# Two layers of attention and gated MLP on one core: where the second layer's weight sums are prepared, and the order of work in its fourth block

## The chip, the core and the metric

The kernel runs on one core of a Trainium2 chip. The core's engines are named as the profile names them: PE (TensorE, matmuls), DVE (VectorE), ACT (ScalarE), POOL (GpSimd) and SP (SyncE, which here issues DMAs). Each engine works through its own instructions in the order of the program and waits for others by semaphores. The metric is the device time of one execution in microseconds (us). Lower is better.

## The reference

```python
def _A_ref(x, wqkv, wo):                       # H = 16 heads, D = 448, Dh = 28
    q, k, v = ...                              # (x @ wqkv) cut in three, by heads
    scores = jnp.einsum("bhqd,bhkd->bhqk", q, k) * (Dh ** -0.5)
    o = jnp.einsum("bhqk,bhkd->bhqd", _softmax(scores), v)
    return o.transpose(...).reshape(B, S, D) @ wo
def _B_ref(x, w_gate, w_up, w_down):           # F = 1792
    return (_sigmoid(x @ w_gate) * (x @ w_up)) @ w_down

x = x + _A_ref(_layernorm(x), A_wqkv, A_wo)    # x is 1 x 2048 x 448, float32
x = x + _B_ref(_layernorm(x), B_w_gate, B_w_up, B_w_down)
x = x + _A_ref(_layernorm(x), A_wqkv, A_wo)    # the same weights again
x = x + _B_ref(_layernorm(x), B_w_gate, B_w_up, B_w_down)
```

## The kernel before, in words

The 2048 tokens are worked in four blocks of 512. A layer goes through four stages: `project` (layer norm, then q, k and v of each block), `attend` (scores, exponentials, products with the values, over 256 chunks: 16 heads by 16 key chunks), `out_project` (the output projection, the additions to x, the next layer norm) and `gated` (the MLP). Numbers in float32 are carried as a high and a low half-precision part, so most products are done as three.

**Two ways of projecting.** In the first layer q and k of a block come from `qk`: seven tiles of 128 features. For each tile PE makes the products (L618) into one of four banks; ACT reads out the high part (L871) and squares it (L874), DVE makes the low part (L872) and a maximum over halves of the squares (L878), SP stores q and k (L881), and PE adds up the squares by heads (L850 for q, L853 for k). That last product is held back by three tiles in a queue called `late`: after the products of the tile with index i come the norm products of the tile i - 3. After each tile `qk` calls a step of the list `fill`, in which other work of the kernel is put by hand. In the second layer the third and fourth block use `qk_sums` instead, a scheme of the Strassen kind on pairs of tiles. It multiplies with sums of quarters of the weight matrix rather than with the quarters themselves. Six tiles are taken as three pairs, `PAIRS_QK = ((0, 1), (4, 5), (2, 6))`; tile 3 is alone (`ALONE`) and is multiplied in the usual way into a bank named "alone". `qk_sums` returns `finish`, which does deferred squares one at a time when it is called with `whole=False`, and otherwise the last norm sums and the maxima over them (`peaks`, L1088).

**The weight sums.** They are prepared while the first layer runs. `read_pairs(js)` loads the float32 columns of the given pairs into a buffer `raws` with four DMAs a pair (L732, L734; POOL's queue) and a memset. The buffer has two halves: pairs 0 and 2 use one, pair 1 the other. `keep_pair(j)` makes the sums (`add_up`, four additions on DVE, L254), their high parts (ACT, L263; or DVE, L261, if it is named as the engine) and their low parts (DVE, L266), and POOL sends the pack to memory (L750), from where the second layer loads it. Pair 2 mixes two scales, so two scalings on DVE (L746) go ahead. Before, pairs 0 and 1 are read in the last steps of the second block's `qk`, and kept after the first and second tile of the third block's. Pair 2 is read after the third block's third tile and kept, all on DVE, at the start of attention.

**The input blocks.** A later block is normalized on DVE, stored by four DMAs to a scratch in memory (`store`, L391) and gathered in turned order by two (`gather`, L399 and L401), both on SP; `ready` then splits it. The fourth block's gather (`b3.gather`) stands at the first tile of the second block's values (`vals(1, ...)`).

**The guard.** After the fourth block's q and k, `guard_of_norms` (in the first layer called within the first tile of `vals(2, ...)`) takes a bound from the peaks, writes a guard row (DVE, L1228) and sends it off on POOL. `worst_of_heads` (L1235 to L1237) makes a flag from it; all engines load the flag and branch on it (L1244). After the branch SP loads the first heads, and the value products of the fourth block's last two tiles are done beside the first scores. DVE reads such a tile out (L1124).

**Attention and what follows.** In attention PE makes scores (L1529), ACT takes exponentials of three chunks at once (L1544), DVE does some by a polynomial, PE multiplies with the values (L1580). `along(c)` is called once a chunk and puts the preparation of other weights in. `out_project` makes six output products (into six banks), adds tails, and then DVE adds the first four tiles to x (`add`, L1713) and takes their statistics; PE's later products need the banks that these additions free.

Of the kernel before, what the change touches and what calls it, by code (L numbers as in the profile page):

```python
# [19 lines left out]
P = 128  # L20
# [101 lines left out]
def interleaved_layers(ctx: ExitStack, tc: tile.TileContext, x_in, wqkv, wo, w_gate, w_up,  # L122
                       w_down, out):
    nc = tc.nc
# [530 lines left out]
    class WeightsQKV:  # L655
# [66 lines left out]
            nc.sync.dma_start(v_parts, self.v)  # L722
            big.put(*self.qk, self.v)

        def read_pairs(self, js):
            self.raws = big.get("raws", [P, 2, 1024])
            self.to_add = len(js)
            for j in js:
                v = self.pair(j)
                for z, i in enumerate(PAIRS_QK[j]):  # L730
                    c = slice(i * P, (i + 1) * P)
                    nc.gpsimd.dma_start(v[:, 0:3, z],  # L732
                                        wqkv[0:384, c].rearrange("(s p) n -> p s n", p=P))
                    nc.gpsimd.dma_start(v[0:64, 3, z], wqkv[384:448, c])  # L734
                nc.gpsimd.memset(v[64:P, 3], 0.0)

        def pair(self, j):
            return self.raws[:, j % 2].rearrange("p (s z n) -> p s z n", s=4, z=2)

        def keep_pair(self, j, engine=None):  # L740
            v, t = self.pair(j), big.get("pack", [P, N_SUMS, P], F16)
            m = [int(i > ALONE) for i in PAIRS_QK[j]]
            by = up[:, m[0]:m[0] + 1]
            if m[0] != m[1]:
                for z in range(2):
                    nc.vector.tensor_scalar(v[:, :, z], v[:, :, z], up[:, m[z]:m[z] + 1], None,  # L746
                                            op0=ALU.mult)
                by = ones[:, 0:1]
            split_sums(t, v, by, engine)
            nc.gpsimd.dma_start(qs_parts[j], t)  # L750
            big.put(t)
            self.to_add -= 1
            if not self.to_add:
                big.put(self.raws)

        def load(self, j):
# [69 lines left out]
    def project(layer, wq, begun):  # L826
# [69 lines left out]
        def qk_sums(b, blk, points, before=None, defer=False):  # L896
# [21 lines left out]
            def at(i):  # L918
                for do in points.get(i, ()):
                    do()  # L920
# [105 lines left out]
            pa.third()  # L1026
            pb.third()
            at(2)
            if before:
                before(False)  # L1030
                before(False)
            pa.c11_c22()
            pb.c11_c22()
            at(3)
            pa.tiles[0].high()
            pa.c21()
            pa.tiles[0].low(pa.one)
# [1 line left out]
            pb.c21()  # L1039
            pb.tiles[0].low(pb.one)  # L1040
            pa.c12()
            if before:
                before()
            pb.c12()
            alone = bank(5 - b % 2, "alone")
            pc = Pair(2, 6)
            pc.first()
            pa.tiles[1].high()
            pa.tiles[1].low(pa.two)
            some(3)  # L1050
# [120 lines left out]
        if layer == 0:  # L1171
            fin = qk(0, blks[0], fill, None)
            vals(0, blks[0], along_values)
            fill = [b2.gather, b3.norm, sq(3, 0, 1), sq(3, 2, 3), idle,
                    lambda: b2.ready(0, 1), lambda: (b2.ready(2, 3), b3.store())]
            fill[4] = lambda: wq.read_pairs((0, 1))
            fin = qk(1, b1, fill, None)
            vals(1, b1, {0: b3.gather, 2: fin})
            add = tell.add
            fin = qk(2, b2, [lambda: wq.keep_pair(0),  # L1180
                             lambda: (wq.keep_pair(1), b3.ready(0, 1)),
                             lambda: (b3.ready(2, 3), wq.read_pairs((2,))), idle, add, add,
                             add], None)
            fin = qk(3, blks[3], [add, add, add], fin)
        else:
            ones_of_values()
            wq.load_usual()
            h2, h3, s3 = b2.half_steps(), b3.half_steps(), b3.squared()
            ready = [lambda kt=kt: b1.ready(kt) for kt in range(4)]
            both = lambda *steps: lambda: [do() for do in steps]  # L1190
            fin = qk_sums(0, blks[0], {0: ready[0:1], 1: ready[1:2], 2: s3[0:1],
                                       4: ready[2:3], 5: ready[3:4] + s3[1:2]})
            vals(0, blks[0], {0: both(s3[2], s3[3], s3[6], h2[0]), 1: both(s3[4], s3[7]),
                              2: both(fin, s3[5], s3[8], s3[9], b3.store),
                              3: both(h2[1], h2[2], b3.gather)})
            fin = qk(1, b1, h2[3:10], None)
            big.put(*wq.qk)
            vals(1, b1, {0: h3[0], 1: both(h3[1], h3[2], fin), 2: both(*h3[3:5]),
                         3: both(*h3[5:7])}, banks=(3, 0, 1, 6))
            fin = qk_sums(2, b2, {0: h3[7:8], 1: h3[8:9], 4: h3[9:10]}, None, True)  # L1200
            fin = qk_sums(3, b3, {}, fin)
        if layer > 0:
            big.put(*wq.held[1:])
            evac[0] = 0
        else:
            both_back(0, 0, 1, SCALE * 2.0 ** -20)
            nc.scalar.reg_load(exp_scale, back.bitcast(I32)[0:1, 0:1])
            nc.vector.tensor_scalar(base2, back[:, 0:1], math.log2(math.e), None, op0=ALU.mult)
# [11 lines left out]
        def guard_of_norms():  # L1220

            fin()
            heads[0].load()
            nc.vector.tensor_reduce(top, peaks, axis=AX.X, op=ALU.max)
            nc.vector.scalar_tensor_tensor(bnd, top[:, 0:1], SLACK, top[:, 1:2], op0=ALU.mult,
                                           op1=ALU.mult)
            nc.gpsimd.tensor_tensor(bnd, bnd, half[0:H, 0:1], op=ALU.pow)
            nc.vector.tensor_scalar(guard, zero, bnd, -1.0 / UNIT, op0=ALU.add, op1=ALU.mult)  # L1228
            nc.gpsimd.dma_start(g_scr[:, 0, :], guard)
            nc.gpsimd.dma_start(g_scr[:, 1, :], zero)  # L1230
            big.put(guard, zero)

        def worst_of_heads():
            pb = bank(4, "bounds")
# [15 lines left out]
        heads[0].load_guard()  # L1250
        heads[1].load()
        heads[1].load_guard()
        if layer == 0:
            wq.keep_pair(2, nc.vector)

        vals(3, blks[3], {}, [2], 0 if layer == 0 else 7)

        def last_values(begun=None):
# [239 lines left out]
                2 if half is None else half]  # L1498
            return self.kt[3][r, k, t * P:(t + 1) * P]

    def attend(layer, values, heads, last_values, gate, keep):
        new_banks()
        heads = list(heads)
        outs = Outputs()
# [87 lines left out]
        def along(c):  # L1592
            nonlocal prepare
            if layer == 0 and c == 2:
                keep()
            if layer == 0 and c == 4:
                prepare = Prepare()
            if prepare:
                prepare.along(c)
# [84 lines left out]
        return outs  # L1684


    def out_project(outs, gate):
        new_banks()
        nc.scalar.activation(warm, warm, AF.Sigmoid)
        nc.scalar.reg_load(gate_scale, back.bitcast(I32)[0:1, 3:4])  # L1690
# [25 lines left out]
        gate.load_gu()  # L1716
        gate.load_usual()
        products(range(6), range(6))
        first.begin()
        tails(range(4))  # L1720
        for t in range(4):
# [499 lines left out]
    for layer in range(LAYERS):  # L2221
        values, heads, last_values = project(layer, wq, begun)
        gate = WeightsGated()
        outs = attend(layer, values, heads, last_values, gate, wq.keep)
        mlp_first = out_project(outs, gate)
        wq = WeightsQKV()

        begun = gated(layer, mlp_first, gate, wq)
# [28 lines left out]
```

## Time and profile before

| what | value |
| --- | --- |
| median of three runs | 1900.61 us (1899.11 to 1901.45) |
| the profiled execution: its time | 1900.84 us |
| its span, first to last instruction | 1898.9 us |
| PE busy | 1882.1 us (99%) |
| DVE busy | 1480.3 us (78%) |
| ACT busy | 1422.5 us (75%) |
| POOL busy | 252.1 us (13%) |
| mean granted clock of PE | 0.998 |

The span is taken by the profiler within the execution; the execution's own time is 1.9 us longer. In a row of a timeline, the first number is the start in us from the span's beginning, the second the duration of the row (of all its instructions together, where it ends on xN), then come the engine, the line of the kernel, the operation, what it writes <- what it reads with the shape, the count, and in square brackets how long the engine had been idle before it and what it waited for. A q behind an engine's name (SPq, ACTq) marks its DMA issues. A row of the waits of PE gives the total wait, the number of waits and the longest. In a window's row the mean granted clock stands behind the busy times of PE, PEld (weight load), DVE, ACT and POOL.

### The profile page before, as it was taken

The numbers are of one execution on the slowest core, as the hardware profiler recorded it, in microseconds if no ns is written. First come the engines' busy times: TensorE is split into PE (matmuls) and PEld (weight loads), VectorE is DVE, ScalarE is ACT, GpSimd is POOL, SyncE is SP. The second block draws the span as 40 slices with busy tenths as digits, with TensorE's granted clock in tenths as the row PEclk, the third lists the DMA queues.
The fourth block names the chain that finished last, engine by engine and source line by source line (L and its number), as shares of the span: only waits on it lengthen the run. The fifth ranks groups of instructions, "written<-read, shape, count | busy, mean of one in ns | idle before, by whom it ended". The sixth has DMA issues, their size and how long they took to land. (4 is left out here: it accounts for less than half of the span.)

```text
span 1898.9 us, 57174 instructions
## 1 busy us (share of the span) xinstructions
PE 1882.1 (99%) x24531; PEld 1365.9 (72%) x24531; DVE 1480.3 (78%) x2988; ACT 1422.5 (75%) x1881; POOL 252.1 (13%) x489
## 2 busy tenths in 40 slices
PE   9999999999999999999999999999999999999999
PEld 4447756655565899999977566667666568999998
DVE  7858989898987887788867577787787688877664
ACT  5559999999993655555557899999999746555541
POOL 3313112122201211112110000000000021111110
PEclk9999999999999999999999999999999999999999
DMA  7775534434332755656573421122120246566553
GB/s 248 255 219 155 137 107 137 114 113 130 110 107 68 255 193 199 244 207 232 184 239 114 107 51 35 44 52 48 30 52 13 75 157 227 201 228 223 212 207 141
DMA packets 117335, 278.70 MB, mean 147 GB/s; under 512 B 14574, under 2 KB 72686, under 8 KB 116944
## 3 DMA queue, kind: packets, MB, share of 16 engines
q0 software_dynamic: 33680, 166.05, 24.2%
q1 hardware_dynamic: 82240, 107.53, 19.7%
q8 instruction: 194, 3.18, 0.7%
q10 hardware_dynamic: 1152, 1.38, 0.3%
q14 instruction: 69, 0.57, 0.1%
HBM read 213.43 MB, written 53.08 MB: 140 GB/s over the span
## 5 line engine op out<-in xcount | busy, mean ns | idle before, releaser
L1544 ACT ACTIVATE prob_s<-sc 128x1536 f32<-128x1536 f32 (+1 forms) x657 | 888.9, 1478 | 15.0 <-PE sc L1529 9.9
L1580 PE MATMUL acc<-prob_s,val_s 128*32 128x256 f32 (+3 forms) x7700 | 577.1, 384 | 1.6 <-issue 1.6
L1529 PE MATMUL sc<-qp_s 114*32 114x512 f16 x7868 | 559.9, 379 | 0.0
L633 PEld LDWEIGHTS <-gu_s 128*128 128x128 f16 x4368 | 426.8, 98 | 45.8 <-PE op L1709 0.7
L1529 PEld LDWEIGHTS <-qp_s 114*32 114x32 f16 x8192 | 283.4, 96 | 196.0 <-issue 85.5
L1580 PEld LDWEIGHTS acc<-prob_s,val_s 128*32 128x32 f32 x7700 | 284.1, 110 | 134.1 <-issue 13.6
L633 PE MATMUL chain<-xwide_s,gu_s 128*128 128x256 f16 x2016 | 247.6, 273 | 0.0
L1889 PE MATMUL dnp<-dn_s,hparts_s 128*128 128x224 f16 x2184 | 246.0, 259 | 0.2 <-DVE x L1907 0.2
L1889 PEld LDWEIGHTS <-hparts_s 128*128 128x128 f16 x2184 | 210.2, 98 | 5.5 <-issue 0.3
L1560 DVE SCALAR_TENSOR_TENSOR power_q<-power_q,expo_q 128x512 f32<-128x512 f32 x243 | 168.2, 692 | 8.3
L1962 ACT COPY one_q<-chain 128x256 f32<-128x256 f32 x224 | 82.3, 371 | 113.9 <-PE chain L633 113.4
L1978 DVE TENSOR_TENSOR one_q<-side,one_q 128x512 f32<-128x512 f32 x112 | 72.1, 686 | 95.8 <-PE side L633 95.6
L633 PE MATMUL side<-xshort_s,gu_s 128*128 128x256 f16 x1120 | 140.6, 273 | 0.0
L1770 POOL DMA_DIRECT2D gu_s<-gu_parts x104 | 56.0, 539 | 428.6 <-PE side L633 425.0
L1609 DVE STREAM_TRANSPOSE oturned_q<-acc 128x512 f32<-128x512 f32 x32 | 22.9, 717 | 100.5 <-PE acc L1580 100.4
L1842 ACT CAST hparts_s<-hsums_q 128x256 f16<-128x256 f32 (+1 forms) x152 | 71.5, 485 | 37.2 <-DVE hsums_q L1854 23.6
L1580 PE MATMUL acc<-power_q,val_s 128*32 128x256 f32 (+3 forms) x300 | 94.2, 396 | 0.0
L633 PE MATMUL side<-xwide_s,gu_s 128*128 128x256 f16 x672 | 91.7, 273 | 0.0
L618 PE MATMUL qkp<-xhl_s,wqk_s 128*128 128x512 f16 x385 | 86.7, 379 | 0.9 <-ACT wqk_s L235 0.6
L1989 ACT ACTIVATE one_q<-one_q 128x512 f32<-128x512 f32 x56 | 35.3, 631 | 63.9 <-DVE one_q L1978 63.6
L1554 DVE TENSOR_SCALAR expo_q<-aside,base 128x512 f32<-128x512 f32 x81 | 60.6, 748 | 22.7 <-PE aside L1529 22.3
L1846 DVE TENSOR_TENSOR hparts_s<-hsums_q,hparts_s 128x256 f16<-128x256 f32 (+1 forms) x152 | 72.8, 519 | 5.9 <-ACT hparts_s L1842 5.9
(262 smaller groups left out, 2398.8 us busy)
## 6 DMA issues: line engine op xcount, KB each, us to landing
gu_s<-gu_parts POOLq DMA_DIRECT2D x104, 800.0 KB, 5.9
dn_s<-dn_parts POOLq DMA_DIRECT2D x42, 784.0 KB, 7.5
qp_s<-qk_scr SPq DMA_DIRECT2D x96, 224.0 KB
gu_parts<-pack_s POOLq DMA_DIRECT2D x14, 800.0 KB, 3.8
xt_scr<-xs_s SPq DMA_DIRECT2D x48, 224.0 KB
xraw_s<-xt_scr SPq DMA_DIRECT2D x12, 768.0 KB
qk_scr<-qkhl_q SPq DMA_DIRECT2D x35, 256.0 KB
qp_s<-qk_scr SPq DMA_DIRECT2D x64, 112.0 KB
```

The lines of the kernel that those rows point to most:

```text
L618: nc.tensor.matmul(pm, w, x, start=(i == 0), stop=(i == len(terms) - 1))
L633: nc.tensor.matmul(pm, a, x, start=(first and i == 0), stop=(i == len(terms) - 1), skip_group_check=True)
L1529: nc.tensor.matmul(ps[32 * j:32 * j + 32, :], hd.k[:, keys], hd.q[:, qb * W:(qb + 1) * W], start=True, stop=True, tile_position=(0, 32 * j))
L1544: nc.scalar.activation(prob[:, 0:n, :], ps[:, 0:n, :], AF.Exp, scale=exp_scale)
L1554: nc.vector.tensor_scalar(y, ps, base2[:, 0:1], -126.0, op0=ALU.mult, op1=ALU.max)
L1560: nc.vector.scalar_tensor_tensor(p, p, c[k], y, op0=ALU.add, op1=ALU.mult)
L1580: nc.tensor.matmul(acc[qb * VC:(qb + 1) * VC, s], v[:, kc % TB, h, :], probs[c * NB + qb][:, s], start=(kc == 0 and a == 0), stop=(kc == N ...
L1842: nc.scalar.copy(to[:, :, 0], a)
L1846: nc.vector.tensor_tensor(to[:, :, 1], a, to[:, :, 0], op=ALU.subtract)
L1889: nc.tensor.matmul(pm, a[:, x, t], w[:, p, y], start=(begin and n == 0 and (j == 0 or alone)), stop=(n == 2), skip_group_check=True)
L1962: nc.scalar.copy(to, pm)
L1978: nc.vector.tensor_tensor(one[m], side[m], one[m], op=ALU.add)
```

## The change

In the first layer the three pairs are handled one by one, each at another place. Pair 0 is read on SP's queue at the second tile of the second block's values, behind the fourth block's gather, and kept as before after the third block's first tile. Pair 1 is read on SP after the fourth block's first tile and kept behind the guard. Pair 2 is read on POOL's queue six chunks before the end of attention and kept in `out_project`, behind the first six output products; its high parts go to ACT. In the second layer the half steps of the fourth block's input are dealt out differently over the steps around it; in the fourth block's `qk_sums` two deferred squares of the third block move behind `at(3)`, the third block's last norm sums and peaks move behind `pc.first()`, and the lone tile takes bank 0 instead of bank 4. The counter that hands out read-out banks starts at 1 instead of 0 behind it.

```diff
-        def read_pairs(self, js):
-            self.raws = big.get("raws", [P, 2, 1024])
-            self.to_add = len(js)
-            for j in js:
-                v = self.pair(j)
-                for z, i in enumerate(PAIRS_QK[j]):
-                    c = slice(i * P, (i + 1) * P)
-                    nc.gpsimd.dma_start(v[:, 0:3, z],
-                                        wqkv[0:384, c].rearrange("(s p) n -> p s n", p=P))
-                    nc.gpsimd.dma_start(v[0:64, 3, z], wqkv[384:448, c])
-                nc.gpsimd.memset(v[64:P, 3], 0.0)
+        def read_pair(self, j, queue=nc.sync):
+            if j != 1:
+                self.raws = big.get("raws", [P, 2, 1024])
+            v = self.pair(j)
+            for z, i in enumerate(PAIRS_QK[j]):
+                c = slice(i * P, (i + 1) * P)
+                queue.dma_start(v[:, 0:3, z], wqkv[0:384, c].rearrange("(s p) n -> p s n", p=P))
+                queue.dma_start(v[0:64, 3, z], wqkv[384:448, c])
+            nc.gpsimd.memset(v[64:P, 3], 0.0)
...
-        def keep_pair(self, j, engine=None):
+        def keep_pair(self, j):
...
-            split_sums(t, v, by, engine)
+            split_sums(t, v, by)
             nc.gpsimd.dma_start(qs_parts[j], t)
             big.put(t)
-            self.to_add -= 1
-            if not self.to_add:
+            if j > 0:
                 big.put(self.raws)
...
             at(2)
+            pa.c11_c22()
+            pb.c11_c22()
+            at(3)
             if before:
                 before(False)
                 before(False)
-            pa.c11_c22()
-            pb.c11_c22()
-            at(3)
...
             pa.c12()
+            pb.c12()
+            alone = bank(0 if before else 5, "alone")
+            pc = Pair(2, 6)
+            pc.first()
             if before:
                 before()
-            pb.c12()
-            alone = bank(5 - b % 2, "alone")
-            pc = Pair(2, 6)
-            pc.first()
...
-            fill[4] = lambda: wq.read_pairs((0, 1))
             fin = qk(1, b1, fill, None)
-            vals(1, b1, {0: b3.gather, 2: fin})
+            vals(1, b1, {0: b3.gather, 1: lambda: wq.read_pair(0), 2: fin})
             add = tell.add
             fin = qk(2, b2, [lambda: wq.keep_pair(0),
-                             lambda: (wq.keep_pair(1), b3.ready(0, 1)),
-                             lambda: (b3.ready(2, 3), wq.read_pairs((2,))), idle, add, add,
+                             lambda: b3.ready(0, 1), lambda: b3.ready(2, 3), idle, add, add,
                              add], None)
-            fin = qk(3, blks[3], [add, add, add], fin)
+            fin = qk(3, blks[3], [lambda: (add(), wq.read_pair(1)), add, add], fin)
...
-            vals(1, b1, {0: h3[0], 1: both(h3[1], h3[2], fin), 2: both(*h3[3:5]),
-                         3: both(*h3[5:7])}, banks=(3, 0, 1, 6))
-            fin = qk_sums(2, b2, {0: h3[7:8], 1: h3[8:9], 4: h3[9:10]}, None, True)
+            vals(1, b1, {0: both(*h3[0:2]), 1: both(h3[2], fin), 2: both(*h3[3:5]),
+                         3: h3[5]}, banks=(3, 0, 1, 6))
+            fin = qk_sums(2, b2, {0: h3[6:7], 1: h3[7:8], 3: h3[8:9], 4: h3[9:10]}, None, True)
...
-            evac[0] = 0
+            evac[0] = 1
...
             big.put(guard, zero)
+            if layer == 0:
+                wq.keep_pair(1)
...
-        if layer == 0:
-            wq.keep_pair(2, nc.vector)
-
         vals(3, blks[3], {}, [2], 0 if layer == 0 else 7)
...
+            if layer == 0 and c == total - 6:
+                wq.read_pair(2, nc.gpsimd)
...
         products(range(6), range(6))
+        if wq:
+            wq.keep_pair(2)
         first.begin()
```

`attend` and `out_project` are handed the object `wq` for this (`out_project` only in the first layer).

More of the change, by code (lines that the diff above doesn't have):

```diff
@@ L1499, in tail, with attend @@
             return self.kt[3][r, k, t * P:(t + 1) * P]
-    def attend(layer, values, heads, last_values, gate, keep):
+    def attend(layer, values, heads, last_values, gate, wq):
         new_banks()
@@ L1594, in along @@
             if layer == 0 and c == 2:
-                keep()
+                wq.keep()
+            if layer == 0 and c == total - 6:
+                wq.read_pair(2, nc.gpsimd)
             if layer == 0 and c == 4:
@@ L1684, in attend, with out_project @@
         return outs
-    def out_project(outs, gate):
+    def out_project(outs, gate, wq):
         new_banks()
@@ L2223, in interleaved_layers @@
         gate = WeightsGated()
-        outs = attend(layer, values, heads, last_values, gate, wq.keep)
-        mlp_first = out_project(outs, gate)
+        outs = attend(layer, values, heads, last_values, gate, wq)
+        mlp_first = out_project(outs, gate, wq if layer == 0 else None)
         wq = WeightsQKV()
```

## The prediction

> **What bounds the kernel.** I read the page first, then its waits of PE, the timelines of PE, DVE, ACT and SP around each edited place, the windows, and the pair buffer's tile view.
>
> ```profile
> span 1898.9 us, 57174 instructions
> PE 1882.1 (99%) x24531; PEld 1365.9 (72%) x24531; DVE 1480.3 (78%) x2988; ACT 1422.5 (75%) x1881; POOL 252.1 (13%) x489
> ```
>
> PE is busy but for 17 us, so an edit can count in three ways: it removes or adds a PE wait, it changes the granted clock, or it moves a stage that another engine paces. Attention is such a stage:
>
> ```profile
> 121.00:131.00 10.00, 6.55 (x47) 2.00 (x43) 4.28 (x10) 4.20 (x3) 0.57 (x1) 0.66 0.96 306
> 300.00:560.00 260.00, 260.00 (x4752) 154.80 (x4748) 233.58 (x458) 259.88 (x194) 50.48 (x86) 1.00 0.40 121
> ```
>
> The columns are length, then busy time of PE, PEld, DVE, ACT, POOL, then granted clock, DMA share, GB/s. In 300 to 560 ACT is busy 259.88 of 260, so a later or earlier start of ACT's exponentials carries through to the end of attention. In 121 to 131 PE works only 6.55 us and the mean clock is 0.66. The waits of PE that the edits touch:
>
> ```profile
> PE vp L643 <- DVE val_s L1124: 3.5, 1, 3.5
> PE qnorm L850 <- DVE sq_q L878: 1.0, 1, 1.0
> PE alone L1010 <- DVE peaks L1088: 0.6, 1, 0.6
> PE side L633 <- DVE one_q L984: 0.6, 1, 0.6
> PE chain L633 <- ACT one_q L968: 0.4, 1, 0.4
> ```
>
> **Part A: pair 2 leaves the start of attention, first layer.** Start, duration, engine, line:
>
> ```profile
> 113.52 0.16 DVE L1236 TENSOR_REDUCE worst<-bounds 1x1 f32<-1x16 f32 x1 [4.14 <-PE bounds L1235]
> 117.64 0.88 DVE L746 TENSOR_SCALAR raws_s<-raws_s,up 128x512 f32<-128x512 f32 x2 [3.71 <-DVEq L1244]
> 124.33 0.62 DVE L1124 TENSOR_SCALAR val_s<-vp 128x448 f32<-128x448 f32 x1
> 125.01 0.53 PE L643 MATMUL vp<-wv_s,xhl_s 128*128 128x448 f16 x1 [3.45 <-DVE val_s L1124]
> 120.96 2.79 ACT L1544 ACTIVATE prob_s<-sc 128x1536 f32<-128x1536 f32 x2 [2.62 <-DMA qp_s<-qk_scr]
> 128.86 1.45 ACT L1544 ACTIVATE prob_s<-sc 128x1536 f32<-128x1536 f32 x1 [5.11 <-PE sc L1529]
> 131.40 4.14 ACT L1544 ACTIVATE prob_s<-sc 128x1536 f32<-128x1536 f32 x3 [1.09 <-DMA qk_parts<-wqk_s]
> 1062.43 4.13 ACT L1544 ACTIVATE prob_s<-sc 128x1536 f32<-128x1536 f32 x3 [2.62 <-PE sc L1529]
> 1066.90 4.14 ACT L1544 ACTIVATE prob_s<-sc 128x1536 f32<-128x1536 f32 x3 [0.33 <-PE sc L1529]
> ```
>
> Pair 2's work (scalings, then L254, L261 and L266) holds DVE from 117.64 to 124.3; only then is the value tile read out (L1124), and PE waits 3.45 us for that bank. A clock of 0.66 over 10 us is 6.8 us at half speed, which slows the matmuls that follow too. The second layer has the same start without the sums: its fourth exponential begins 1066.90 - 1062.43 = 4.47 us after its first, against 131.40 - 120.96 = 10.44 here. The change makes the first layer like the second: 5.97 us earlier. Pair 1 now sits on DVE behind the guard, in an idle stretch before the flag; DVE is idle there for 4.14 us up to 113.52, that is from 109.4, and the pair's present length is 4.3 us (below), so the flag comes 0.2 us later. **A = -5.8**, bounds -6.0 (the whole difference) and -4.5 (the wait and its clock shortened, but a transfer late for the fourth exponential by the 1.09 us of the row and a little more).
>
> **Part B: pair 0's reads move from POOL to SP, behind the fourth input block's gather.**
>
> ```profile
> 63.16 0.53 POOL L734 DMA_DIRECT2D raws_s<-in_A_wqkv_dram  x1
> 65.94 3.52 SPq L391 DMA_DIRECT2D xt_scr<-xs_s  x4
> 73.83 0.38 SPq L399 DMA_DIRECT2D xraw_s<-xt_scr  x1
> 74.26 0.49 SPq L401 DMA_DIRECT2D xraw_s<-xt_scr  x1
> 615.41 3.02 SPq L391 DMA_DIRECT2D xt_scr<-xs_s  x4
> 621.68 0.39 SPq L399 DMA_DIRECT2D xraw_s<-xt_scr  x1
> DMA to landing us min/median/max: 2.9/5.1/9.5
> 72.18 0.49 ACT L263 ACTIVATE pack_s<-raws_s,up 128x256 f16<-128x256 f32 x1
> 73.43 1.39 ACT L263 ACTIVATE pack_s<-sums_q,up 128x512 f16<-128x512 f32 x2 [0.76 <-DVE sums_q L254]
> 72.52 0.42 DVE L254 TENSOR_TENSOR sums_q<-raws_s 128x256 f32<-128x256 f32 x1
> 77.44 0.28 DVE L878 TENSOR_TENSOR sq_q<-sq_q 128x256 bf16<-128x256 bf16 x1
> 77.64 0.42 DVE L254 TENSOR_TENSOR sums_q<-raws_s 128x256 f32<-128x256 f32 x1
> ...
> 81.46 0.47 DVE L266 SCALAR_TENSOR_TENSOR pack_s<-raws_s,up,pack_s 64x256 f16<-64x256 f32 x1
> 80.42 0.27 PE L850 MATMUL qnorm<-sq_q,ind 128*128 128x256 bf16 x1
> 84.11 0.27 PE L850 MATMUL qnorm<-sq_q,ind 128*128 128x256 bf16 x1 [1.04 <-DVE sq_q L878]
> ```
>
> Today the last read is issued from POOL at 63.16 and pair 0's work starts at 72.18 on ACT and 72.52 on DVE without waiting. In the new order SP issues the reads after the gather (L399, L401), and the gather waits on SP until the four stores (L391) have landed, to 73.83; in the twin at 615.41 the gather goes 3.25 us after the stores' last issue, so with the POOL reads out of the way it may go at 69.46 + 3.25 = 72.7. Two gather issues and four reads of 0.4 to 0.5 us each put the last read's issue at 75.4 to 76.5. By the tile view its landing takes 2.9 at least and 5.1 in the middle: 78.3 to 81.6, and I take 80.0. But the pair's work keeps its place in the program, so ACT and DVE both stop in front of it, and all that is queued behind stops with them: the third block's second tile (its read-out L871, L872, its square L874, L878). Its square is done at 77.72, 5.2 us after DVE began the pair, so then at 85.2. PE has run four more tiles ahead by then and needs that square at 80.42: a wait of 85.3 - 80.42 = 4.9 us. Against this the wait of 1.04 at 84.11 goes, since pair 1's 4.3 us (77.64 to 81.93) no longer lie between the next tiles. The clock: at 121 to 131 the delay of 5.97 was 3.45 of wait and so 2.5 of half speed behind it; of the 6.8 us at half speed 5.0 lay on work and 1.8 in the wait. A wait 1.45 us longer takes as much more of that stretch into itself, and 0.7 less is lost: 1.8. **B = 4.9 - 1.0 + 1.8 = +5.7**, bounds +2.2 (reads at 78.3, a wait of 3.2, full clock) and +8.0 (reads at 81.6, a wait of 6.5, 2.5 lost).
>
> The row for the clock is the window 121 to 131: a wait of 3.45 us was enough. [...]
>
> Pair 1's reads on SP at the fourth block's first step come some five tiles of 2.5 us after 84.11, near 96, and are used from 109.4 on; the longest landing is 9.5. Pair 2's on POOL are issued six chunks before attention ends, and used when DVE goes idle, 7.71 us before 587.68: nothing for either. What hides them is that wide gap; without it a late read costs its delay once. SP's stores of q and k (L881) stand behind pair 0's reads and start some 2 us later, while ACT stands still anyway.
>
> **Part C: pair 2 in the first layer's output projection.**
>
> ```profile
> 584.28 1.28 ACT L1689 ACT_TABLE_LOAD   x1 [9.48 <-DMA ot_s<-ohl_q]
> 585.57 0.20 ACT L1689 ACTIVATE warm<-warm 128x1 f32<-128x1 f32 x1
> 587.68 0.68 DVE L1713 SCALAR_TENSOR_TENSOR x<-op,back,x 128x448 f32<-128x448 f32 x1 [7.71 <-PE op L1709]
> 593.50 2.43 DVE L1713 SCALAR_TENSOR_TENSOR x<-op,back,x 128x448 f32<-128x448 f32 x4
> 595.93 0.35 PE L643 MATMUL op<-wout_s,ot_s 128*128 128x448 f16 x1
> ```
>
> DVE is idle for 7.71 us before 587.68, and the scalings and additions (0.88 and four of 0.42, 2.5 us) fit. But the high parts go to ACT, which is free only after its DMA issues, the table and the warm-up: 585.77. Four highs are one of 0.49, two in 1.39 and one more of that size, 0.7: 2.5 us; the last three lows on DVE, by the row at 81.46 up to 0.47 each, follow by some 1.3. DVE is free at 589.6 instead of 587.68, 1.9 late. The third of the four additions at 593.50 frees the bank that PE's product at 595.93 takes: done at 593.50 + 3 x 0.61 = 595.3, a cover of 0.6. **C = 1.9 - 0.6 = +1.3**, bounds 0 (ACT overlaps better) and +2.5 (a later normalization and turn also come late).
>
> **Part D: second layer, fourth block.** The lone tile's bank waits today for the third block's peaks:
>
> ```profile
> 1039.68 0.50 PE L1010 MATMUL alone<-xwide_s,wsums_s 128*128 128x256 f16 x3 [0.64 <-DVE peaks L1088]
> ```
>
> Another bank and later peaks take away this 0.64. The deferred squares behind at(3) let DVE finish the side sums sooner (the 0.6 of the waits, at 1036.73), and the shifted half steps free ACT for the 0.4 at the third block's start. Together -1.6, and new waits can take their place, up to +0.6. **D = -1.6.**
>
> **Sum:** -5.8 + 5.7 + 1.3 - 1.6 = -0.4 on the profiled execution's 1900.84, which is 0.2 over the median of 1900.61: **1900.4 us**. A measurement of this kernel can tell about 0.2%, 3.8 us, from no change.
>
> **Rivals.** *Faster: the third block's wait is short.* If the reads land by 78.0, the wait is 78.0 + 5.3 - 80.42 = 2.9, under the 3.45 that is known to lower the clock, and B is 2.9 - 1.0 = 1.9: 1900.84 - 5.8 + 1.9 + 1.3 - 1.6 = 1896.6. For it: the transfers between 64 and 74 get lighter. Against: the earliest issue, 75.4, and the shortest landing, 2.9, give 78.3. Chance 0.20.
>
> *Slower: the reads queue behind the gather's data,* sent from the same queue just ahead. With the longest landing of the tile view, 9.5, the reads come at 76.0 + 9.5 = 85.5, the wait is 10.4, B is 9.4 and with 1.8 of half speed 11.2: 1905.9. It decides from a landing at 84.0 on, where B stands 4.0 over my value and the sum at the 0.2%. For it: the landing times are spread by a factor of three. Against: the POOL reads that met other loads still had a middle of 5.1. Chance 0.17.
>
> *Slower too: attention's start stays late.* The row at 131.40 names a transfer, and the DMA share is 0.96 in 121 to 131. If the fourth exponential waited for a transfer and not for PE, only the wait's 1.1 to 1.5 us come back: A = -1.3 and 1904.9. Against: the second layer's 4.47 with the same head loads, and PE's own wait, which ends on DVE. Chance 0.05.
>
> That the change doesn't do what it says at attention's start would need pair 2's work to stay there, and the diff takes the call out.
>
> **How the numbers follow.** My forecast has 0.58. Its own range: ends of B (2.2 to 8.0) with the other terms' smaller ones put together at random, 1897.5 to 1903.5. With half of each outer case taken in, the range is 1895.8 to 1905.5. Faster by over 0.2% (under 1896.8): 0.20. Slower (over 1904.4): 0.17 + 0.05 = 0.22. Same: 0.58.
>
> **What would show it.** Right: no PE wait on L1124 and a clock near 1.00 in 121 to 131; the fourth exponential 4.5 us after the first; ACT and DVE waiting for the DMA of the pair buffer in front of L263 and L254 near 80, and PE on L850 for about 4.9 us, with a lowered clock after; a PE wait of 1 to 2 us on L1713 at the out-projection; the waits on L1088 and L984 gone. Wrong: a wait at L850 under 3 us or over 7 us; an exponential that still waits for a transfer at attention's start; a third block without any wait for the reads.

## The result and the profile after

The changed kernel took 1909.34 us by its median of six executions (1906.35 to 1909.98), the kernel before 1900.71 beside it: a ratio of 1.0041, 95% interval 1.0028 to 1.0054, so 0.4% slower. 1900.4 was forecast, with a range up to 1905.5. The changed kernel's profiled execution took 1906.35 us with a span of 1904.6, against 1900.84 and 1898.9 before. The medians thus lie 8.6 us apart and the profiled executions 5.5; the account below is of the profiled ones.

The page's waits of PE, after (total, number, longest):

```profile
PE qnorm L847 <- DVE sq_q L875: 6.9, 1, 6.9
PE turn L562 <- DVE xn_s L362: 4.9, 2, 3.6
PE vp L643 <- DVEq L1241: 1.9, 1, 1.9
PE op L643 <- DVE x L1709: 0.9, 1, 0.9
```

The wait for the value tile's read-out (3.5), those for the lone tile's peaks and for the side and chain sums (0.6, 0.6, 0.4) are gone. In their place stand four waits, of which the forecast had two: the third block's norm product (6.9) and the output projection's 0.9. It had neither the one at the branch (1.9) nor the new one at the turns (3.6; the 2.2 that the row had before stood at the program's first turns, near 8 us, and is 1.2 there now).

Both kernels do the same number of matmuls, 24,531, and but for a few that change places in the second layer in the same order. So each matmul's start can be set against that of its partner, the matmul of the same rank, and the difference, after less before, shows where time went and came from:

```
place (start before, us)                       after - before, us
end of the second block (66)                        -0.6
third block, second norm product (80.42)            +6.5
third block, after half speed (82.5)                +8.4
from there to the fourth block's end (84 to 113)    +7.6 to +7.4
values, behind the branch (117.90)                  +9.1
attention's start (130.20)                          +3.2
attention, 150.13                                   +1.4
output projection, before its first wait            +1.1
eleventh output product (595.93)                    +2.1
first turn (597.63) / sixteenth turn (599.27)       +5.9 / +7.9
second layer, third block (1010.70)                 +8.2
second layer, lone tile (1039.68)                   +6.1
last matmul (1895.14)                               +5.7
```

**The third block.** Timelines of SP, ACT, DVE and PE, after:

```profile
74.02 0.38 SPq L399 DMA_DIRECT2D xraw_s<-xt_scr  x1
...
76.79 0.50 SPq L732 DMA_DIRECT2D raws_s<-in_A_wqkv_dram  x1
80.60 0.51 ACT L263 ACTIVATE pack_s<-raws_s,up 128x256 f16<-128x256 f32 x1 [8.91 <-DMA raws_s<-in_A_wqkv_dram]
81.63 0.42 DVE L254 TENSOR_TENSOR sums_q<-raws_s 128x256 f32<-128x256 f32 x1 [9.61 <-DMA raws_s<-in_A_wqkv_dram]
86.90 0.37 PE L847 MATMUL qnorm<-sq_q,ind 128*128 128x256 bf16 x1 [6.90 <-DVE sq_q L875]
87.06 4.82 PE L618 MATMUL qkp<-xhl_s,wqk_s 128*128 128x512 f16 x11
91.83 2.54 PE L618 MATMUL qkp<-xhl_s,wqk_s 128*128 128x512 f16 x11
```

ACT and DVE stood 8.9 and 9.6 us in front of pair 0's data, and PE then 6.9 us in front of the second tile's squares. The eleven matmuls behind the wait took 4.82 us, the next eleven 2.54: the first tile ran at half speed (the clock records have 0.5 from 84.85 to 91.68).

**Attention's start** came out as the second layer's does: the fourth exponential 4.4 us behind the first (10.44 before), and no wait at L1121.

```profile
130.14 4.14 ACT L1538 ACTIVATE prob_s<-sc 128x1536 f32<-128x1536 f32 x3 [4.43 <-PE sc L1523]
134.54 10.85 ACT L1538 ACTIVATE prob_s<-sc 128x1536 f32<-128x1536 f32 x8 [0.27 <-PE sc L1523]
127.01 0.36 PE L643 MATMUL vp<-wv_s,xhl_s 128*128 128x448 f16 x1 [1.88 <-DVEq L1241]
```

The last of the three rows is the new wait at the branch: PE had passed it and waited for DVE to do the same.

**The output projection** is where the forecast missed most. Timelines of POOL, DVE and PE, after:

```profile
590.79 0.56 POOL L748 DMA_DIRECT2D qs_parts<-pack_s  x1 [43.59 <-issue]
602.02 0.18 POOL L552 TENSOR_SCALAR rs<-mv 128x1 f32<-128x1 f32 x1 [10.66 <-issue]
602.92 0.51 DVE L362 TENSOR_SCALAR xn_s<-x,mv,rs 128x448 f32<-128x448 f32 x1 [4.40 <-POOL rs L554]
597.98 0.35 PE L643 MATMUL op<-wout_s,ot_s 128*128 128x448 f16 x1 [0.93 <-DVE x L1709]
603.49 4.00 PE L562 MATMUL turn<-ident,xn_s 128*128 128x128 f32 x16 [3.65 <-DVE xn_s L362]
```

POOL sends pair 2's pack (L748) and then does nothing for 10.66 us, though the first statistics of the next layer norm have lain ready since 591.8. "issue" says that no wait is seen. DVE's scalings (L362) wait for POOL, PE's turns for DVE. The four tiles' statistics then come out of POOL one by one, 0.95 us apart, and PE's clock records have half speed from 603.68 to 607.09, so the 16 turns take 4.00 us; they took 1.91 before. The profile before had POOL at L552 at once:

```profile
589.42 0.19 POOL L552 TENSOR_SCALAR rs<-mv 128x1 f32<-128x1 f32 x1 [49.75 <-DVE mv L550]
597.63 1.91 PE L562 MATMUL turn<-ident,xn_s 128*128 128x128 f32 x16
```

The trace's instruction records tell what lies in the gap: two MODIFY_POOL_CONFIG instructions stand ahead of L552 in both kernels. Before they came at 539.74, right behind POOL's last DMA of attention, with 50 us of idle time to follow; after they came at 591.42, behind pair 2's pack. POOL's last other such pair was at 188.9, before the all-reduce in attention's preparation (L1432). What POOL does behind such a pair no record shows. That it changes its code there is my guess and was not shown; as the expectations use the word, the pair and the gap behind it are called a change of code below.

### The profile page after: what moved, and what is told of

Read it like the earlier page. It is cut to its first block, busy times and chain, and to the rows that moved or that the text cites. A ratio compares the mean times of both kernels' runs of the same rounds, so it can differ in the third digit from the quotient of the medians.

```text
span 1904.6 us, 57187 instructions
## 1 busy us (share of the span) xinstructions
PE 1883.3 (99%) x24531; PEld 1365.9 (72%) x24531; DVE 1479.3 (78%) x2984; ACT 1424.6 (75%) x1885; POOL 248.8 (13%) x481
## 5 line engine op out<-in xcount | busy, mean ns | idle before, releaser
L1844 DVE TENSOR_TENSOR hparts_s<-hsums_q,hparts_s 128x256 f16<-128x256 f32 (+1 forms) x152 | 72.7, 517 | 5.9 <-ACT hparts_s L1840 5.9
```

The lines of the kernel that those rows point to most:

```text
L1844: nc.vector.tensor_tensor(to[:, :, 1], a, to[:, :, 0], op=ALU.subtract)
```

## The experiments

Two theories went into the first four runs: that the losses in the third block and the output projection come from two separate orders of work (the reads behind the gather; POOL's change of code behind the pack), or that they come from what was moved, wherever it is put. Further down, theory 1 and theory 2 are those of the expectation just above.

**POOL's change of code, early.** One more small arithmetic instruction on POOL in attention:

```diff
                 wq.read_pair(2, nc.gpsimd)
+                poke = cpool.tile([P, 1], F32, name="poke", tag="poke", bufs=1)
+                nc.gpsimd.memset(poke, 1.0)
+                nc.gpsimd.tensor_scalar(poke, poke, EPS, XS ** -2, op0=ALU.add, op1=ALU.mult)
```

> The changed kernel with one small arithmetic instruction more on POOL (a 128x1 addition and multiplication on a scratch tile), right after pair 2's reads, six chunks before attention ends. Theory 1: in the changed kernel POOL stands still from 591.9 to 602.0 because after the all-reduce of 195 us it has to change its code before its next arithmetic (two MODIFY_POOL_CONFIG instructions at 591.4), and pair 2's pack DMA now holds that change back until 590.8; the early instruction lets the change happen at about 547 behind attention. Then the four statistics on POOL run as they come, PE's wait of 3.65 in front of the turns (603.49) and the slow turns (4.00 instead of 1.91) go, the 0.9 at L1709 stays: 5.7 us less than the changed kernel, 1900.7 in the state of its profiled execution and about 1903.5 by its median. Theory 2: POOL waits for its own pack DMA, which lands at 599.1 among the loads for the MLP; then the early instruction changes nothing (1906 to 1910) and POOL's gap at 592 to 602 stays.

Measured: 1902.54 us (1900.22 to 1904.51), ratio to before 1.0010 (1.0000 to 1.0019), where the changed kernel has 1.0041: 5.9 us less by the ratios. POOL's timeline:

```profile
546.89 0.10 POOL L1593 MEMSET poke<- 128x1 f32 x1
558.58 0.64 POOL L1594 TENSOR_SCALAR poke<-poke 128x1 f32<-128x1 f32 x1 [11.58 <-DVE power_q L1552]
590.46 0.74 POOL L748 DMA_DIRECT2D qs_parts<-pack_s  x1 [31.24 <-issue]
591.60 0.18 POOL L552 TENSOR_SCALAR rs<-mv 128x1 f32<-128x1 f32 x1 [0.40 <-DVE mv L550]
```

The 11.58 us now lie at the small instruction, which needs no data (the DVE instruction that the row names has nothing to do with it), and L552 follows the same pack by 0.4 us. PE's wait at the turns is gone, and by the matmul starts 5.9 us are won there. (At the last matmul this profile leads by 3.8; part of what is lost in between goes to a new wait of 1.2 for the second layer's weights, at L1101.) So the gap belongs to the first arithmetic after the all-reduce and not to the pack's landing: theory 1. A memset (L1593) does not bring it about: it ran at 546.89, ahead of the 11.58 us, with no gap in front of it.

**Pair 0's reads on POOL again.**

```diff
+            fill[4] = lambda: wq.read_pair(0, nc.gpsimd)
             fin = qk(1, b1, fill, None)
-            vals(1, b1, {0: b3.gather, 1: lambda: wq.read_pair(0), 2: fin})
+            vals(1, b1, {0: b3.gather, 2: fin})
```

> The changed kernel with pair 0's four reads issued by POOL in the second block's fifth step, as before, and not on SP behind the gather. Theory 1: the order on SP alone makes the third block's wait. The reads land by about 66, ACT and DVE start pair 0 near 71.5, PE's waits of 6.9 (with 2.0 of half speed behind) and the 1.0 at that place are both gone: 8.4 to 9.0 us less than the changed kernel, of which 0.6 may come back at the second block's norm products, so 1898 in the state of the profiled execution and about 1901 by its median. Theory 2: it is pair 0's work in front of the second tile, whatever brings its data; then a wait of 3 us or more stays at the norm product and less than 5 us are won.

Measured: 1900.53 us (1898.36 to 1902.77), ratio 0.9999 (0.9989 to 1.0008), 8 us less than the changed kernel. ACT starts pair 0 at 71.89 without a wait, and no norm product of the third block waits:

```profile
71.89 0.49 ACT L263 ACTIVATE pack_s<-raws_s,up 128x256 f16<-128x256 f32 x1
80.14 0.27 PE L847 MATMUL qnorm<-sq_q,ind 128*128 128x256 bf16 x1
594.70 4.26 PE L562 MATMUL turn<-ident,xn_s 128*128 128x128 f32 x16 [3.25 <-DVE xn_s L362]
```

Theory 1, and the 1.0 at the third norm product that was there before is gone too. The turns still wait: the two losses are separate.

**Both edits together.**

> Both edits above together: pair 0 read by POOL in the second block, and POOL's early instruction. If the two losses are independent and the rest of the change keeps its gains (attention's start and course -6.2 by the two profiles' PE offsets, the second layer -2.2, the output projection +0.9), the kernel takes 1900.7 - 6.2 - 2.2 + 0.9 = 1893 us, and the spread of 3 us between executions of the changed kernel, if it hangs on one of the two waits, is gone. If the losses cover each other, it stays above 1896.

Measured: 1896.00 us (1892.37 to 1896.55), ratio 0.9973 (0.9963 to 0.9984), so faster than before by 0.27%. The losses nearly add up (5.9 and 8.0 apart, 12.9 together). The 1893 was missed by 3; the profile shows 1.8 us of it in the first twelve microseconds, where PE's clock stood lower than in the kernel before (0.89 against 1.00 in 0 to 15 us), and 1.0 in the first layer's MLP, where PE now waits 0.9 for weights (gu_s). Window 0 to 15 us of this kernel (clock 0.89):

```profile
0.00:15.00 15.00, 10.99 (x43) 6.01 (x44) 7.34 (x21) 5.51 (x12) 8.46 (x26) 0.89 0.81 270
```

and of the same kernel with SP's reads, below (1.00):

```profile
0.00:15.00 15.00, 11.23 (x51) 5.37 (x52) 9.06 (x25) 7.32 (x14) 8.79 (x28) 1.00 0.84 274
```

No edit touches that place. The clock records have half speed from 8.19 to 11.61 here, behind a wait of 2.16 us for DVE at the first turns; in the other kernel that wait was 1.79, and no half speed followed. Below, the kernels are therefore compared by their profiles' matmul starts from the second block on; medians of a few executions may carry this start too.

**The second layer's edits alone.** The kernel before with the edits of `qk_sums`, the half steps and the counter, and nothing of the weight sums.

> The kernel before with only the second layer's edits (half steps dealt out anew, deferred squares behind at(3), last norm sums behind pc.first(), lone tile in bank 0, counter at 1); the weight sums stay where they were. Theory 1: the three PE waits of the fourth and third block there (0.64, 0.58, 0.39) go and nothing takes their place: 1.6 to 2.2 us less than before, 1898.5 to 1899.1. Theory 2: new waits take their place: 1900 to 1901.

Measured: 1899.51 us (1897.10 to 1900.57), ratio 0.9991 (0.9981 to 1.0001). The interval takes in no change, so the median alone decides nothing; the profile's last matmul comes 1.2 us earlier. All three waits are gone. One new wait stands at the third block's values (the row below), another of 0.6 at the second layer's first values, for weights from memory, so this is between the two theories:

```profile
1011.30 0.35 PE L643 MATMUL vp<-wv_s,xhl_s 128*128 128x448 f16 x1 [0.53 <-DVE peaks L892]
```

**SP's queue or its order.** Pair 0's reads on SP, but ahead of the store and the gather, in the kernel with both edits:

```diff
-            fill[4] = lambda: wq.read_pair(0, nc.gpsimd)
+            fill[4] = lambda: wq.read_pair(0)
```

> The kernel with both edits (pair 0 read by POOL in the second block, POOL's early instruction), but pair 0's reads are issued by SP at that same place, ahead of the fourth block's store and gather, instead of by POOL. Theory 1: it was the place behind the gather that made the third block's wait, not SP's queue: no wait over 1 us at the third block's second norm product, and the time stays within 1.5 us of the kernel with both edits (1896.0 by its median); the stores and the gather behind the reads start some 2 us later. Theory 2: SP's queue itself is too full there: the reads push the store, the gather and the fourth block's input back, and 3 us or more of wait return, at 1899 or over.

Measured: 1894.87 us (1892.66 to 1895.13), ratio 0.9967 (0.9954 to 0.9979). No wait at the third block. At the end of the second block the two profiles lie 2.5 us apart, and from there on this changes by no more than 1.2. It was the place behind the gather, not SP.

**Pair 2's highs on DVE** in the output projection, in the kernel with both edits (`keep_pair` takes an engine again):

```diff
-            wq.keep_pair(2)
+            wq.keep_pair(2, nc.vector)
```

> The kernel with both edits, and pair 2's four high parts in the output projection made by DVE instead of ACT. Theory 1: the 0.9 to 1.0 us that PE waits at the eleventh output product comes from DVE's 3.85 us of waiting for ACT's highs; with the highs on DVE (0.35 + 0.88 + 0.48, 1.7 us) its work runs through in some 7.3 us, is done near the first additions, and PE's wait goes: 0.9 us less, 1895.1. Theory 2: DVE, not ACT, is late there in any case: the wait stays or grows, 1896 to 1897.

Measured: 1892.92 us (1890.33 to 1894.21), ratio 0.9959 (0.9944 to 0.9973). DVE, from the first scaling to the last low, and then the first addition:

```profile
571.04 0.88 DVE L744 TENSOR_SCALAR raws_s<-raws_s,up 128x512 f32<-128x512 f32 x2
...
577.22 0.47 DVE L266 SCALAR_TENSOR_TENSOR pack_s<-raws_s,ones,pack_s 64x256 f16<-64x256 f32 x1
578.75 0.68 DVE L1713 SCALAR_TENSOR_TENSOR x<-op,back,x 128x448 f32<-128x448 f32 x1 [1.06 <-PE op L1709]
```

It takes 6.7 us, ends 1.06 us before PE's output is there, and the wait of 1.0 at the eleventh product is gone. The profile shows 1.2 us won there (its offset against the kernel with both edits goes from -3.6 to -4.8); the rest of its lead is the start and small differences along attention. Theory 1.

**Pair 1's pack behind the branch.** In the kernel with both edits, POOL sends the pack after the branch:

```diff
-            nc.gpsimd.dma_start(qs_parts[j], t)
+            self.t = t
+            if j != 1:
+                self.send_pair(j)
...
+        if layer == 0:
+            wq.send_pair(1)
         vals(3, blks[3], {}, [2], 0 if layer == 0 else 7)
```

> The kernel with both edits, and pair 1's pack (819 KB) sent by POOL after the branch on the flag instead of right before it. In the changed kernel DVE takes 4.9 us from its branch to its next instruction (122.04 to 126.93), in the kernel before 2.9 (114.58 to 117.43), and PE waits 1.9 us for it. Theory 1: the pack's transfer, which starts as the engines jump, delays the fetching of DVE's code; sent later, DVE's restart takes about 3 us and the 1.9 us of wait go, 1894.2 by the median. Theory 2: the 4.9 us belong to where DVE's code lies after the change; then the wait stays at 1.9 and the time at 1896.

Measured: 1891.68 us (1891.20 to 1893.60), ratio 0.9953 (0.9936 to 0.9970). DVE's records have 2.9 us from its branch to its next instruction (113.46 to 116.33) and 4.9 in the kernel with both edits (115.06 to 119.95), and PE's wait is gone. By the matmul starts 1.7 us are won at the branch; the two ratios' intervals overlap, so the profile carries this and not the medians. The DMA view shows why; the rows that it calls instruction are read here as the packets that bring code to the engines. The kernel with both edits, 115 to 117 us:

```profile
DMA packets 93, 0.60 MB, mean 298 GB/s; under 512 B 0, under 2 KB 0, under 8 KB 93
q0 software_dynamic: 93, 0.60, 74.8%
```

and 117 to 119 us:

```profile
q8 instruction: 1, 0.02, 2.9%
q14 instruction: 2, 0.02, 1.9%
```

For two microseconds behind the branch only pack packets move (q0), and the three packets of code come after them; the last, on q8, runs from 118.30 to 119.23, and DVE goes on at 119.95. With the pack sent later, 113.5 to 115.2 us, they come alone and sooner; the one on q8 runs from 114.68 to 116.04, and DVE goes on at 116.33:

```profile
DMA packets 3, 0.03 MB, mean 19 GB/s; under 512 B 0, under 2 KB 0, under 8 KB 0
q8 instruction: 1, 0.02, 5.0%
q14 instruction: 2, 0.02, 3.0%
```

Theory 1: in these two runs the code waited behind the pack's 819 KB, 4.9 us to DVE's next instruction with the pack ahead and 2.9 without.

**The changed kernel once more.**

> The changed kernel itself, on the same chip as the three others, with a new profile: 1906 to 1910 (ratio to before 1.004). In its first profile the third block's wait was 6.9 us and PE's wait at the turns 3.65, with PE at full speed behind the turns; its other executions were 1 to 3.6 us longer. If POOL's change of code is what varies, the new profile shows a longer gap at POOL before L552 or half speed behind the turns; if it is the reads, a longer wait at the third block's second norm product.

Measured: 1908.69 us (1906.85 to 1910.85), ratio 1.0043 (1.0029 to 1.0058). Its profile, of 1906.85, has the same waits (6.5, 3.6, 1.9, 0.9) and its matmuls start within 0.7 us of the first profile's. Neither of the two expected causes of the spread shows in it. Both profiles fell on the shortest execution of their set; most others had a mean clock of 0.996 where the profiled ones had 0.997. A slow start as seen above would fit, but no profile of a longer execution is there to show it.

**All four edits.** Pair 0 read by POOL, the early instruction, the highs on DVE, the late pack.

> All four edits together: pair 0 read by POOL in the second block, POOL's early instruction, pair 2's highs on DVE in the output projection, pair 1's pack sent after the branch. By the profiles' PE offsets the last two took 0.9 and 1.9 us off the kernel with the first two, and touch different places: some 2.8 us less than that kernel at the same start, a profile near 1889 and a median of 1890 to 1892 (ratio to before 0.994 to 0.995). If the two gains overlap, 1892 to 1894.

Measured: 1892.98 us (1891.73 to 1899.11), ratio 0.9960 (0.9945 to 0.9976); no better than the late pack without the highs (1891.68; the intervals overlap), and over the 1890 to 1892 expected. The profile is 1.5 us ahead of that kernel's at the output projection, and 0.9 behind it after the second layer's first value products:

```profile
972.24 1.30 PE L1106 MATMUL vp<-wv_s,xwide_s 128*128 128x448 f16 x6 [1.93 <-DMA wv_s<-v_parts]
```

The second layer's first value products wait for weights from memory. In the other kernels' profiles this wait is 1.2 us at most or absent. The first layer's MLP has such a wait too (gu_s): 0.6 to 0.9 us in five of the kernels that reach it earlier than the changed one, and none in the profiles before and after. So part of what is won earlier is lost again in front of weights that have not landed yet.

**Pair 2 back at attention's start,** in the kernel with all four edits; read by POOL after the third block's third tile:

```diff
+            wq.keep_pair(2, nc.vector)
         vals(3, blks[3], {}, [2], 0 if layer == 0 else 7)
...
-        if wq:
-            wq.keep_pair(2, nc.vector)
```

> The kernel with all four edits, but pair 2 back where it was: read by POOL after the third block's third tile, and kept on DVE between the branch and the value tile at the start of attention. It measures alone what moving pair 2 out of attention's start brings. Theory 1 (the prediction's part A): PE's wait of 3.5 us before L643 and the half speed behind it return, and attention starts and runs later by 5.8 to 7.8 us, nothing comes back in the output projection: 1896.5 to 1899. Theory 2: most of A's gain came from elsewhere, or attention takes the late start up: less than 3 us more than the kernel with all four.

Measured: 1896.88 us (1894.98 to 1899.94), ratio 0.9979 (0.9970 to 0.9987). The wait of 3.4 us at the value tile is back, and ACT's exponentials break off again (fourth against first: 130.04 - 120.78 = 9.3 us):

```profile
120.78 2.79 ACT L1547 ACTIVATE prob_s<-sc 128x1536 f32<-128x1536 f32 x2 [2.79 <-DMA qp_s<-qk_scr]
128.29 1.45 ACT L1547 ACTIVATE prob_s<-sc 128x1536 f32<-128x1536 f32 x1 [4.71 <-issue]
130.04 5.52 ACT L1547 ACTIVATE prob_s<-sc 128x1536 f32<-128x1536 f32 x4 [0.30 <-DMA qp_s<-g_scr]
```

By the matmul starts, without the 1.6 us that this run is behind up to attention, it is 5.6 us later at 150 us and 6.2 at the end of attention: theory 1 as far as attention goes. Of this 1.0 us is won back in the MLP and 2.1 at the second layer's start, at both of which this kernel does not wait for its weights. At the last matmul 2.3 are left; the medians differ by 3.9.

This run also shows the gap behind the pair with less traffic. Nothing of pair 2 is read in front of POOL's early instruction, the DMA share in the gap is 0.40 (0.71 in the changed kernel's, 591.42 to 602.02), and the gap is shorter:

```profile
545.09 0.18 POOL L1602 TENSOR_SCALAR poke<-poke 128x1 f32<-128x1 f32 x1 [6.93 <-issue]
```

## Why the prediction was wrong

The direction was wrong: no change was forecast, and the kernel is slower. The terms against the table of matmul starts of the profiled executions; 3 us more between the medians stay unexplained, as no profile of a longer execution shows them:

```
term                              forecast   measured
A  attention's start and course     -5.8       -6.5   (+1.5 at the branch, -8.0 behind it)
B  third block                      +5.7       +7.6
C  output projection                +1.3       +6.8
D  second layer                     -1.6       -2.2
sum (profiled executions)           -0.4       +5.7   (spans; executions +5.5)
```

**The step that failed is in part C.** The prediction counted pair 2's instructions on DVE and ACT, and found that DVE would be 1.9 us late with a cover of 0.6. That much came: DVE's first addition at 590.27 instead of 587.68 (of which 1.0 is the later end of attention; 1.6 late, then), and PE's 0.93. But the step also issues a DMA on POOL, and the prediction did not ask what is queued behind it there. It was POOL's change of code, which took 10.7 us now; before, its pair came at the beginning of POOL's 49.75 us of idle time (539.74), and nothing waited for it. The row with those 49.75 us was in the profile before; that the pair was in them only its instruction records show. Moved behind the pack, it cost PE 3.65 us at the first turn and 2.1 in the slow turns. The early instruction takes this away and leaves the 0.9. The trace shows the gap behind the pair and no instruction that fills it; the return to ordinary arithmetic took 10.7 us here (591.4 to 602.0), and 6.9 to 11.6 in the kernels with the early instruction.

**Part B had the mechanism right and two sizes off.** The gather went at 74.02 and not at 72.7, since the stores did not land sooner without POOL's reads (73.83 with them); four read issues and the gather's two ended at 77.3, and DVE had its data at 81.6, the upper end given, where I took 80.0. That is 1.6 of the wait's 6.9 against 4.9. PE was 0.6 early, which lengthens the wait and leaves the end where it is. Half speed took 2.0 (forecast 1.8), and 0.8 came back at the next norm product (forecast 1.0).

**Part A had the right size for the wrong sum, by luck.** The start brought 5.9, as forecast from the second layer (5.97), and attention's course another 2, which the forecast did not have and whose cause no run takes apart. But the flag was to cost 0.2, and the branch cost 1.5: the prediction named the work of pair 1 in front of the flag and not its pack, whose transfer held up DVE's code behind the branch (4.9 us to DVE's next instruction, 2.9 with the pack sent later). It is the same omission as in part C. The rival by which attention's start stays late did not come.

**Part D** lost three waits and got back a smaller one. In the changed kernel it gave 2.2 us, alone 1.2 (there the two new waits, of 0.5 and 0.6, count against it).

**Two slips of the working.** The own range begins at 1897.5, but B at its lower end of 2.2 alone gives 1896.9; and 63.16 is the last read of pair 1, pair 0's was issued on POOL at 60.27. Neither touches the step that failed.

**The rivals.** The faster one, a short wait in the third block, did not come. The slower rival named the third block and a landing at 84 or later. The kernel came out slower with a landing at 81.6, by POOL's gap, which no rival had. Without that gap the changed kernel has a ratio of 1.0010, what the forecast called no change. On the clock: the wait of 6.9 us went with half speed (from 84.85 to 91.68), and so did that of 3.65 at the turns (a mean clock of 0.81 in 600 to 606, 0.79 in the second profile), while that of 1.9 at the branch did not (1.00 in 125 to 130). The wait of 3.25 in the kernel with pair 0's reads on POOL, shorter than the 3.45 that the forecast went by, was followed by half speed too (593.62 to 600.45).

## What to carry to other kernels

When a step is moved, list its DMAs with the queue of each, and for each queue ask what stands behind the DMA there, now that it waits for the moved work: here POOL's gap of 10.66 us behind its pair of instructions and the packets of code behind DVE's branch (4.9 us instead of 2.9) counted, though the groups of instructions don't show them. An engine's long idle time may be hiding a cost that appears only when something is put into it: here POOL's 49.75 us, at whose beginning the pair came. And a read put behind a transfer that itself waits inherits that wait (the gather waited to 74.02, the reads came after it); where its user sits in the middle of an in-order stream, everything behind the user inherits it too (8.9 us on ACT, 9.6 on DVE, then 6.9 on PE).

## What the hardware showed that I had not expected

- POOL's first ordinary arithmetic after an all-reduce came behind a gap: of 10.66 us in the changed kernel (DMA share 0.71 in it), 11.58 with the early instruction, 11.43 with both edits, and 6.93 with pair 2 back at attention's start (0.40). That the traffic makes the difference is likely, but was not tested alone. Memsets and DMA issues ran without such a gap (with the early instruction, pair 2's four reads and two memsets from 543.90 to 546.99, right before the 11.58).
- DVE's restart behind the branch took 4.9 us with an 819 KB pack just sent, 2.9 us without, on otherwise equal code.
- The program's start ran with a lower clock in the kernel with both edits (0.89 in 0 to 15 us, against 1.00 in the kernel before and with SP's early reads), 1.8 us for the same matmuls.
- The clock records of the profiles before and after have three stretches of half speed up to the last matmul: 123.42 to 130.25 before, 84.85 to 91.68 and 603.68 to 607.09 after, so 6.83, 6.83 and 3.41 us. The first began 1.87 us into a wait of PE of 3.45, the second 4.85 into one of 6.90, the third 0.19 behind one of 3.65. A wait of 2.17 in the profile before (5.55 to 7.72) was not followed by half speed, while one of 2.16 in the kernel with both edits was (8.19 to 11.61).
